# First transform stage of the convolution kernels on four 64x64 tiles of TensorE

## Chip, cores, metric

One core of one Trainium2 chip. The time is device microseconds of one execution, the median of several runs; it is lower when better. The engines are TensorE (PE; its weight loads are listed apart as PEld), VectorE (DVE), ScalarE (ACT) and GpSimd (POOL); SyncE (SP) issues every DMA. Each engine works through its own list of instructions in order and waits on semaphores of the others.

## What is computed

Two state-space convolutions of the same input, mixed by a gate per time step. Length L = 2048, D = 512 channels, N = 128 states. Cut to what matters:

```python
def reference(A_u, ..., gate_w):
    x = A_u                                             # (1, 2048, 512)
    g = sigmoid((x * gate_w).sum(-1, keepdims=True))
    # A: K[d, l] = Re sum_n C dB exp(dt (A_re + i A_im) l)
    # B: K[d, l] = 2 Re sum_n C dt exp(dt (-exp(log_A_real) + i A_imag) l)
    # each: y = irfft(rfft(K, 2L) * rfft(u, 2L))[:L] + u * Dskip
    a = _A_ref(x, ...)
    b = _B_ref(x, ...)
    return g * a + (1 - g) * b
```

## The kernel before

The channels go in four blocks of 128 (`q`), each in two halves of 64 (`v` = 0 to 7). For each `v` there are eight chunks: 16 channels of one of the two convolutions.

A chunk (`chunk`) makes the tables of exponentials on POOL (lines 647 to 670), sines and cosines on ACT (678 to 680), multiplies them on DVE (686 to 701), and PE contracts over the 128 states (`products`, line 715): per channel 32 x 64 values of the convolution kernel, four channels below each other on 128 partitions. Two chunks fill one PSUM bank of 512 columns; ACT copies it to the tile `K` (738).

`put` (line 751) is then the first stage of the Fourier transform, and the function that the change touches. `K` holds, for each of 8 groups of 64 columns, four channels of 32 rows. The tile `w1` (128 x 2 x 128) holds the 32-point transform four times, block by block: a channel's 32 rows meet only the 32 columns of its own block in each of the two parts `d` (cosines, sines), and everything else in `w1` is zero. Each matmul takes 64 columns of `K` as weights and streams 128 columns of `w1`; the two `d` go to the upper and lower half of the output's partitions. Sixteen matmuls fill a pair of PSUM banks (a tile `sd` of 1024 columns, of which there are three), and two copies on DVE or ACT (line 769) bring them to the transform's tile `F`. Four puts make one `F`; there are 32 puts for the kernels (8 `v` of four). The same function transforms the input itself (16 puts, `stage1_u`, from tiles `U` loaded by DMA).

The second stage is line 785 for the input (its results are copied to `z` at 836 and stored in DRAM, `ud`) and line 800 for the kernels; DVE multiplies the two spectra (883), line 898 is the first stage back (64x64 tiles; copied out at 908 and stored in DRAM, `wt`), and line 950 the last, with the gate in its weights (`wg`). Line 993 sums the gate.

What sets the order: the program's operations are not written in sequence. `Plan.run` orders them by a list schedule with a cost for each operation, a due time (tables `TO`, `LAG`, `FSP`, `AN` and so on), free buffers, and for PE a count of instructions in blocks of 256 (`nbytes`, `IFETCH`); the result is a fixed order for every engine. The bits of `EV` and `EU` say which copy of a put goes to DVE (1) or ACT (0), those of `ZU` and `OE` the same for lines 836 and 961/963.

Of the kernel before, what the change touches and what calls it, by code (L numbers as in the profile page):

```python
# [15 lines left out]
D = 512  # L16
NJ, NS = 32, 64
NV = 8
EV = (206, 37, 9, 69, 20, 76, 130, 96)
EU = (253, 223, 202, 103)  # L20
NQ = 4
NCH = 128
NCK = 16
CHUNKS = ((1, 0), (1, 1), (0, 0), (0, 1), (1, 2), (1, 3), (0, 2), (0, 3))
ZU = (85, 125, 85, 48)
PI = math.pi
TWO32 = 4294967296.0
MAGIC = 12582912.0
# [20 lines left out]
GXD = -5.97  # L49
WLD = 11.63  # L50
LAT = {'T': 0.25, 'A': 0.16, 'V': 0.13, 'G': 0.1, 'D': 1.8}
SWITCH = 0.262
TO = (-3.549, -2.629, 0.024, 2.065, 2.702, 4.345, 4.478, 5.927)
LAG = (-1.572, 1.521, 5.972, -3.631, -5.595, -0.093, -15.199, 4.578)
FSP = (-5.044, 9.977, -10.056, 9.928, 7.18, 10.492, 27.495, -2.472)
FL = (5.005, -9.739, 0.3, -7.997)
YSP = (5.177, -6.259, 8.434, -10.145)
UDS = (-4.854, -10.697, -1.47, -1.248)
USP = (5.775, 19.204, 11.776, -6.458)
GD = -12.752  # L60
GSP = 3.036
GWD = -0.281
TXD = -8.835
TWD = 0.073
UAHEAD = -2.124
UPRE = -5.856
FPRE = -2.78
AN = (-6.526, -8.563, -6.831, -12.505, 1.282, 0.999, -2.599, 15.084)
PT = (-10.796, -0.506, 0.169, -0.007)
PC = (-14.288, -17.548, -13.941, -6.07)  # L70
PO = (-7.807, -2.333, -1.426, 1.94, -2.186, -4.121, 4.064, 1.206)
AO = (3.36, -1.366, 2.265, -0.998, -5.989)
CX = 1.593
CA = 7.577
CV = 6.128
CK = 1.86
CE = 0.094
CS = -1.059
FW = -4.653


def _flat(t):
# [27 lines left out]
class Plan:  # L110
# [6 lines left out]

    def op(self, eng, cost, due, fn, r=(), w=(), func=None, nbytes=0, after=(), hold=()):
        o = Op()
        o.eng, o.cost, o.due, o.fn, o.func, o.nbytes = eng, cost, round(due, 6), fn, func, nbytes  # L120
        o.deps, o.bufs = set(after), []
        for items, wr in ((r, False), (w, True)):
            for it in items:
                b, reg = it if isinstance(it, tuple) else (it, None)
                for p, preg, pw in b.log:
                    if p is not o and (wr or pw) and _meet(reg, preg):
                        o.deps.add(p)
                if wr and reg is None:
                    b.log = []
                b.log.append((o, reg, wr))  # L130
                if b not in o.bufs:
                    o.bufs.append(b)
                    b.left += 1
        o.unit = self.unit
        for b in hold:
            o.bufs.append(b)
            b.left += 1
        self.ops.append(o)
        return o

    def run(self):
# [15 lines left out]
        while n < len(self.ops):  # L157
            nxt = 1e30
            for e in at:
# [76 lines left out]
def gated_s4_mix(ctx: ExitStack, tc: tile.TileContext, ins: dict, out: bass.AP):  # L236
    nc = tc.nc
    V, G, A, T = nc.vector, nc.gpsimd, nc.scalar, nc.tensor
# [7 lines left out]
    op = pl.op  # L246
# [49 lines left out]
    for x in range(2):  # L296
        for i in range(2):
            op(
                "A", 1.0, GXD,
                lambda x=x, i=i: A.copy(  # L300
# [3 lines left out]
                r=[raw_g], w=[(GwB, ((2 * x + i, 2 * x + i + 1),))],  # L304
# [35 lines left out]
    w1 = cst.tile([P, 2, P], F32, tag="w1", name="w1")  # L340
    w1B, w1s = Buf(None), Buf("z")
# [36 lines left out]

    op("V", 0.6, WLD, turn_last, w=[wlB, WB])

# [213 lines left out]
    def chunk(v, i, due):  # L594

        k, g = CHUNKS[i]
        q = v // 2
        d = prm[q]
# [4 lines left out]
        x, E, QD, sn, cs = (Buf(t) for t in ("x", "E", "QD", "sd", "sd"))  # L603
# [5 lines left out]
        if i % 4 == 0:  # L609
# [14 lines left out]
                r=[d["pi"], tmB], w=[gh],  # L624
# [6 lines left out]
                r=[d["fi"]], w=[gh],  # L631
# [3 lines left out]
        def turns():  # L635
# [17 lines left out]
            r=[d["pi"], tmB], w=[(x, h0)],  # L653
# [11 lines left out]
        def above():  # L665
# [9 lines left out]
        e = due + CA  # L675
# [6 lines left out]
        e = due + CV  # L682
# [4 lines left out]
            r=[sn, (E, ((0, 1),)), (E, ((2, 3),))], w=[(QD, h0), (QD, ((2, 3),))],  # L687
# [4 lines left out]
            r=[sn, (E, h1)], w=[(QD, h1)],  # L692
# [6 lines left out]
            r=[cs], w=[(E, ((0, 2),))],  # L699
# [5 lines left out]
        kg, K = kgs[0], Kt[v]  # L705
        ko = 256 * odd

        def products():
# [24 lines left out]
            nbytes=132 if odd else 128,  # L733
# [14 lines left out]

        return b.v("p (h m e) -> p h m e", h=NCH // 2, m=NJ, e=2)

    def put(F, K, items, pos, due, bits):

        B, bs = pair()

        def mms():
            for g in range(8):
                for d in range(2):
                    T.matmul(  # L758
                        bs[g // 4]()[64 * d : 64 * d + 64, 128 * (g % 4) : 128 * (g % 4) + 128],
                        K()[:, 64 * g : 64 * g + 64],  # L760
                        w1[:, d, :],
                        start=True, stop=True,
                    )

        op("T", 1.9, due, mms, r=[items, w1B], w=[B], hold=[F], nbytes=64)
        for h in range(2):

            def evict(h=h, e=V.tensor_copy if bits >> h & 1 else A.copy):
                e(F.t[:, 1024 * pos + 512 * h : 1024 * pos + 512 * h + 512], bs[h]())  # L769

            v1 = bits >> h & 1
            c0 = 32 * pos + 16 * h
            op("V" if v1 else "A", 0.6 if v1 else 0.51, due, evict, r=[B], w=[(F, ((c0, c0 + 16), allm))])

    def ms(ug, y):

# [33 lines left out]
    def stage1_u(q, due):  # L810
        F = Ft["u", q] = Buf("F")
        for h in range(2):
            t = Buf("U")
            for i in range(2):
                op(
                    "D", 0.5, due - UAHEAD, lambda t=t, h=h, i=i: DMA(t.t[:, 512 * i : 512 * i + 512], ins["u1"][q, 2 * h + i]),
                    w=[(t, ((2 * i, 2 * i + 2),))], nbytes=262144, hold=[F],
                )
            for i in range(2):
                put(  # L820
                    F, lambda t=t, i=i: t.t[:, 512 * i : 512 * i + 512], (t, ((2 * i, 2 * i + 2),)), 2 * h + i, due,
                    EU[q] >> 4 * h + 2 * i,
                )

    ulast = []
# [1 line left out]
    def stage2_u(q, due):  # L827

        for ug in range(4):
# [4 lines left out]

            def evict(t=t, b=b, e=V.tensor_copy if ZU[q] >> ug & 1 else A.copy):
                e(
# [3 lines left out]

            v1 = ZU[q] >> ug & 1
            op("V" if v1 else "A", 1.13 if v1 else 1.01, dm, evict, r=[b], w=[t])
# [78 lines left out]
    def final(q, due):  # L921

        for pr in range(2):
# [15 lines left out]
            for b in range(2):  # L939
# [236 lines left out]
```

## Time and profile before

| | us |
|---|---|
| median of 3 runs | 520.14 (516.91 to 524.86) |
| the profiled execution | 514.1 |
| its span, first to last instruction | 511.9 |
| mean granted clock of PE | 0.93 |

The profile is of one execution. Busy time is that of an engine's instructions; matmul ends are modelled, so PE busy is not PE at its peak. "PEclk" is the clock that PE was granted, 1.00 being full. A row "idle before, releaser" tells how long an engine stood still before instructions of a group and whose event ended it; "issue" means that it waited for nothing the profile shows. The chain is followed back from the last instruction, at each step to what released it. The next lines are of the page: busy share in 40 equal slices, in tenths.

```profile
PE   4578798797787998668957898499969969999806
...
POOL 4654598596797899996997999959969999930000
PEclk9999899999868999979978999899989979999958
```

POOL is the fullest from the seventh slice to the 35th; the clock dips in some ten places.

### The profile page before, as it was taken

How to read it: one execution, taken by the hardware profiler on the slowest of the kernel's cores; microseconds unless marked ns; L12 is line 12 of the kernel's file. 1: busy time of each engine (PE TensorE's matmuls, PEld its weight loads, DVE VectorE, ACT ScalarE, POOL GpSimd, SP SyncE). 2: the span in 40 equal slices, each digit the busy share in tenths (PEclk: the TensorE clock that was granted, in tenths of full speed). 3: DMA queues.
4: the chain of work that ended last, by engine and by line, in shares of the span. 5: the costliest groups of instructions: out<-in, count | busy, mean ns of one | idle time of the engine just before them, and what ended most of it. 6: DMA issues, size and time to landing. Idle time of an engine off the chain costs nothing.

```text
span 511.9 us, 22739 instructions
## 1 busy us (share of the span) xinstructions
PE 406.6 (79%) x10096; PEld 363.5 (71%) x10096; DVE 390.8 (76%) x502; ACT 390.9 (76%) x590; POOL 380.8 (74%) x334
## 2 busy tenths in 40 slices
PE   4578798797787998668957898499969969999806
PEld 3577787696677887557846787498858858888706
DVE  5845698879766999979965998969949987965300
ACT  5958679798669988898997888987988877762201
POOL 4654598596797899996997999959969999930000
PEclk9999899999868999979978999899989979999958
DMA  8659968747744254315575565724533686536982
GB/s 307 149 152 271 237 174 238 190 100 184 198 147 127 85 147 142 104 40 151 165 237 191 140 188 156 270 107 108 145 83 86 173 256 213 149 86 186 314 202 85
DMA packets 64512, 85.50 MB, mean 167 GB/s; under 512 B 5792, under 2 KB 38944, under 8 KB 64032
## 3 DMA queue, kind: packets, MB, share of 16 engines
q1 hardware_dynamic: 64416, 84.07, 56.8%
q8 instruction: 79, 1.29, 1.0%
q14 instruction: 17, 0.14, 0.1%
HBM read 50.49 MB, written 33.59 MB: 164 GB/s over the span
## 4 chain that ended last, share of the span: by engine, by line
PE 32%; DVE 21%; DMA 14%; ACT 13%; issue 9%; POOL 8%; SPq 3%; DVEq 0%; ACTq 0%; POOLq 0%
PE sd L758 9%; PE sd L898 5%; PE ps L800 4%; PE ps L715 4%; DVE QD L686 4%; PE ps L950 4%; DVE E L696 3%; DVE z L883 3%; DMA ud<-z 3%; DMA F<-in_c_t 3%; DMA out<-st 2%; PE sd L785 2%; ACT sd L680 2%; DMA U<-in_u 2%; DVE F L769 2%
## 5 line engine op out<-in xcount | busy, mean ns | idle before, releaser
L666 POOL TENSOR_TENSOR E<-AB 128x1024 f32<-128x1024 f32 x64 | 125.4, 1960 | 0.0
L883 DVE TENSOR_TENSOR z<-ps,U 128x1024 f32<-128x1024 f32 x64 | 77.7, 1217 | 21.2 <-PE ps L800 15.3
L898 PE MATMUL sd<-z,Tx 64*64 64x128 f32 x2048 | 71.9, 278 | 22.5 <-DVE z L883 13.3
L647 POOL TENSOR_TENSOR x<-pi,c_tm 128x512 int32<-128x512 int32 x64 | 68.0, 1063 | 25.1 <-ACT sd L680 25.1
L658 POOL TENSOR_TENSOR E<-AB 128x512 f32<-128x512 f32 x64 | 68.7, 1074 | 21.8 <-PE ps L715 12.4
L686 DVE TENSOR_TENSOR QD<-sd,E 128x1024 f32<-128x1024 f32 x64 | 77.8, 1215 | 9.0 <-ACT sd L678 5.0
L715 PE MATMUL ps<-E 128*32 128x64 f32 x2048 | 68.1, 229 | 18.7 <-DVE E L701 8.8
L758 PE MATMUL sd<-w,K 128*64 128x128 f32 x1024 | 71.1, 297 | 11.8 <-ACT K L738 7.0
L696 DVE TENSOR_TENSOR E<-sd,E 128x1024 f32<-128x1024 f32 x64 | 77.7, 1214 | 2.1 <-ACT sd L680 2.0
L800 PE MATMUL ps<-F,Gw 128*128 128x128 f32 x512 | 75.3, 289 | 4.7 <-DVE z L883 3.9
L898 PEld LDWEIGHTS sd<-z,Tx 64*64 64x64 f32 x2048 | 56.5, 134 | 30.8 <-DVE z L883 12.8
L678 ACT ACTIVATE sd<-x 128x1024 f32<-128x1024 int32 x64 | 65.8, 1028 | 13.8 <-DVE QD L691 5.4
L758 PEld LDWEIGHTS sd<-w,K 128*64 128x64 f32 x1024 | 62.9, 150 | 16.5 <-ACT K L738 7.5
L800 PEld LDWEIGHTS ps<-F,Gw 128*128 128x128 f32 x512 | 63.4, 192 | 13.5 <-issue 6.7
L715 PEld LDWEIGHTS ps<-E 128*32 128x32 f32 x2048 | 50.3, 114 | 30.0 <-issue 15.8
L680 ACT ACTIVATE sd<-x 128x1024 f32<-128x1024 f32 x64 | 65.9, 1030 | 6.4 <-DVE QD L691 3.0
L679 ACT ACTIVATE x<-x 128x1024 f32<-128x1024 int32 x64 | 67.8, 1059 | 1.3
L638 POOL TENSOR_TENSOR x<-gh 128x512 int32<-128x512 int32 x64 | 68.6, 1072 | 0.1
L715 PE MATMUL ps<-QD 128*32 128x64 f32 x2048 | 66.6, 226 | 1.0 <-issue 1.0
L908 ACT COPY st<-sd 128x512 f32<-128x512 f32 x60 | 35.2, 587 | 26.5 <-PE sd L898 15.9
L769 DVE COPY F<-sd 128x512 f32<-128x512 f32 x45 | 29.7, 685 | 31.7 <-PE sd L758 25.1
L715 PEld LDWEIGHTS ps<-QD 128*32 128x32 f32 x2048 | 52.1, 115 | 1.2 <-issue 1.2
(109 smaller groups left out, 640.1 us busy)
## 6 DMA issues: line engine op xcount, KB each, us to landing
U<-ud SPq DMA_DIRECT2D x64, 256.0 KB, 4.1
wt<-st SPq DMA_DIRECT2D x60, 256.0 KB, 3.7
F<-wt SPq DMA_DIRECT2D x14, 1024.0 KB, 7.8
ud<-z SPq DMA_DIRECT2D x32, 256.0 KB, 3.6
U<-in_u SPq DMA_DIRECT2D x16, 256.0 KB, 4.8
ud<-z SPq DMA_DIRECT2D x32, 128.0 KB, 3.5
U<-in_uT SPq DMA_DIRECT2D x16, 256.0 KB, 4.0
out<-st SPq DMA_DIRECT2D x16, 256.0 KB, 2.4
```

Source lines behind the costliest of these rows:

```text
L638: G.tensor_tensor(xi()[:, :, 1, :].rearrange("n c (a b) -> n c a b", a=4), t[:, :, 0:4].unsqueeze(3).to_broadcast([P, NCK, 4, 8]), t[:, :, ...
L647: lambda: G.tensor_tensor(xi()[:, :, 0, :], d["piv"]()[:, k, ch, 0].unsqueeze(2).to_broadcast([P, NCK, NJ]), tm[:, 0:NJ].unsqueeze(1).to_b ...
L658: G.tensor_tensor(Ev()[:, :, 0, :].rearrange("n c (a b) -> n c a b", a=4), A1()[:, ca, ::-1].unsqueeze(3).to_broadcast([P, NCK, 4, 8]), BB ...
L666: G.tensor_tensor(Ev()[:, :, 1:3, :].rearrange("n c w t -> n c (w t)"), AA()[:, ca].rearrange("n c w a -> n (c w) a").unsqueeze(3).to_broa ...
L680: op("A", 1.03, e, lambda: A.activation(bv(cs), wv(qv(x)), AF.Sin, bias=HALF_PI, scale=-SCL), r=[x], w=[cs], func="S")
L686: lambda: V.tensor_tensor(ev(QD)[:, :, 0::2, :], bv(sn).rearrange("n w c t -> n c w t"), Ev()[:, :, 0::2, :], ALU.mult),
L696: lambda: V.tensor_tensor(Ev()[:, :, 0:2, :], bv(cs)[:, 0].unsqueeze(2).to_broadcast([P, NCK, 2, NJ]), Ev()[:, :, 0:2, :], ALU.mult),
L715: T.matmul(K4[32 * b : 32 * b + 32, gg, :], ev(QD if w else E)[:, c, 2, :], ev(QD if w else E)[:, c, 0:2].rearrange("n h t -> n (h t)"), s ...
L758: T.matmul(bs[g // 4]()[64 * d : 64 * d + 64, 128 * (g % 4) : 128 * (g % 4) + 128], K()[:, 64 * g : 64 * g + 64], w1[:, d, :], start=True, ...
L800: T.matmul(b.v("p (k m h e) -> p m k h e", k=2, m=4, h=32, e=2)[:, mm], Gw[:, m, :], Fv(F)[:, :, m, :].rearrange("p (k h) e -> p k h e", k=2),
L883: lambda Z=Z, b=b, U=U, y=y: V.tensor_tensor(Z.t.rearrange("p (w k n) -> p w k n", w=2, k=2), b.v("p (k n) -> p k n", k=2, n=256).unsqueez ...
L898: T.matmul(bs[x]()[64 * o : 64 * o + 64, 128 * mp : 128 * mp + 128].rearrange("p (k c) -> p k c", k=2), Tx[p, 1 - w, 8 * ug + 4 * y + 2 * ...
```

## The change

Four things. First, `put` has a form for the kernels (`wide` false) that leaves out the zero blocks: 64 rows of `K` (two channels) against the 64 x 64 block of `w1` that is not zero for them. Per put there are 32 matmuls with 64 rows, 64 weight columns and 64 streamed columns where there were 16 with 128 rows, 64 and 128; the two row halves `h` go to two PSUM banks. Second, each of the two copies then takes one bank, and writes every other run of 64 columns of `F` instead of 512 in a row. The input's puts (`wide` true) stay as they were. Third, the planner's cost of a kernel put goes from 1.9 to 1.05 and its instruction count from 64 to 128, and every cost on PE is multiplied by 1.06 (`PEF`). Fourth, all due times and the bits that deal copies to DVE and ACT are drawn anew, so that the order of all engines changes.

```diff
-EV = (206, 37, 9, 69, 20, 76, 130, 96)
-EU = (253, 223, 202, 103)
+EV = (195, 180, 18, 203, 16, 192, 174, 115)
+EU = (223, 255, 19, 123)
...
-ZU = (85, 125, 85, 48)
+ZU = (81, 119, 86, 56)
...
+PEF = 1.06
...
-OE = (12, 7, 0, 0)
+OE = (12, 7, 8, 8)
...
-LAG = (-1.572, 1.521, 5.972, -3.631, -5.595, -0.093, -15.199, 4.578)
+LAG = (-0.365, 2.001, 8.288, -0.64, -4.356, 1.669, -10.725, 7.648)
...
-        o.eng, o.cost, ... = eng, cost, ...
+        o.eng, o.cost, ... = eng, cost * (PEF if eng == "T" else 1.0), ...
...
-        put(Ft[v], lambda: K.t, K, pos, due + CS, EV[v] >> 2 * pos)
+        put(Ft[v], lambda: K.t, K, pos, due + CS, EV[v] >> 2 * pos, False)
...
             for g in range(8):
-                for d in range(2):
-                    T.matmul(
-                        bs[g // 4]()[64 * d : 64 * d + 64, 128 * (g % 4) : 128 * (g % 4) + 128],
-                        K()[:, 64 * g : 64 * g + 64],
-                        w1[:, d, :],
-                        start=True, stop=True,
-                    )
-
-        op("T", 1.9, due, mms, r=[items, w1B], w=[B], hold=[F], nbytes=64)
+                for h in range(1 if wide else 2):
+                    for d in range(2):
+                        if wide:
+                            T.matmul(
+                                bs[g // 4]()[64 * d : 64 * d + 64, 128 * (g % 4) : 128 * (g % 4) + 128],
+                                K()[:, 64 * g : 64 * g + 64], w1[:, d, :], start=True, stop=True,
+                            )
+                        else:
+                            T.matmul(
+                                bs[h]()[64 * d : 64 * d + 64, 64 * g : 64 * g + 64],
+                                K()[64 * h : 64 * h + 64, 64 * g : 64 * g + 64],
+                                w1[64 * h : 64 * h + 64, d, 64 * h : 64 * h + 64],
+                                start=True, stop=True,
+                            )
+
+        op("T", 1.9 if wide else 1.05, due, mms, ..., nbytes=64 if wide else 128)
...
-                e(F.t[:, 1024 * pos + 512 * h : 1024 * pos + 512 * h + 512], bs[h]())
+                f = F.t[:, 1024 * pos : 1024 * pos + 1024]
+                if wide:
+                    e(f[:, 512 * h : 512 * h + 512], bs[h]())
+                else:
+                    e(f.rearrange("p (g h x) -> p g h x", g=8, h=2)[:, :, h], bs[h]().rearrange("p (g x) -> p g x", g=8))
```

How the order moves, at three places. In these lists a row is a run of like instructions with their number; `sd_102` and the like are a buffer and its copy, `64x128` is the output of one matmul, and line numbers after 747 are about 1 to 15 higher in the changed kernel (758 becomes 761 for the input and 766 for the kernels, 769 becomes 779 and 781, 785 becomes 800, 800 becomes 815, 898 becomes 913).

PE at the start, before: from the input's second load to the first products of the tables (line 715).

```order
L758 MATMUL sd_101<-w_114,U_83 64x128 x16
L758 MATMUL sd_100<-w_114,U_83 64x128 x16
L785 MATMUL sd_101<-F_66,Gw 128x2x64 x8
L785 MATMUL sd_102<-F_67,Gw 128x2x64 x8
L715 MATMUL ps_98<-E_73 32x64 x4
L715 MATMUL ps_98<-QD_76 32x64 x4
```

The same place after.

```order
L761 MATMUL sd_101<-w_114,U_83 64x128 x16
L761 MATMUL sd_100<-w_114,U_83 64x128 x16
L800 MATMUL sd_102<-F_66,Gw 128x2x64 x8
L800 MATMUL sd_101<-F_67,Gw 128x2x64 x8
L800 MATMUL sd_100<-F_67,Gw 128x2x64 x8
L800 MATMUL sd_101<-F_67,Gw 128x2x64 x8
L716 MATMUL ps_98<-E_73 32x64 x4
L716 MATMUL ps_98<-QD_76 32x64 x4
```

Two more groups of the input's second stage stand ahead of the first products, and the last of them writes `sd_101`, which the second has to be copied out of.

PE behind the last products, before: the last kernel's last put and the start of its second stage.

```order
L725 MATMUL ps_98<-dskip,c_id 128x8
L898 MATMUL sd_100<-z_80,Tx 64x128 x16
L758 MATMUL sd_101<-w_114,K_79 64x128 x16
L800 MATMUL ps_99<-F_66,Gw 128x2x64 x4
L800 MATMUL ps_98<-F_67,Gw 128x2x64 x4
L898 MATMUL sd_102<-z_81,Tx 64x128 x16
L800 MATMUL ps_99<-F_67,Gw 128x2x64 x4
L898 MATMUL sd_100<-z_80,Tx 64x128 x16
L950 MATMUL ps_98<-F_68,wg 32x128 x32
```

And after.

```order
L726 MATMUL ps_98<-dskip,c_id 128x8
L913 MATMUL sd_101<-z_81,Tx 64x128 x16
L766 MATMUL sd_102<-w_114,K_79 64x64 x32
L815 MATMUL ps_99<-F_67,Gw 128x2x64 x4
L815 MATMUL ps_98<-F_66,Gw 128x2x64 x4
L913 MATMUL sd_100<-z_80,Tx 64x128 x16
L815 MATMUL ps_99<-F_66,Gw 128x2x64 x4
L913 MATMUL sd_101<-z_81,Tx 64x128 x16
L965 MATMUL ps_98<-F_68,wg 32x128 x32
```

Here nothing moved but the put itself: 32 matmuls of 64x64 in place of 16 of 64x128.

DVE at the last chunks, before: copies of puts (769) among the tables' products (686 to 701).

```order
L769 COPY F_67<-sd_102 128x512
L686 TENSOR_TENSOR QD_77<-sd_100,E_73 128x16x2x32
L691 SCALAR_TENSOR_TENSOR QD_77<-sd_100,E_73 128x16x32
L701 TENSOR_TENSOR E_73<-sd_102,E_73 128x16x32
L696 TENSOR_TENSOR E_73<-sd_102,E_73 128x16x64
L883 TENSOR_TENSOR z_80<-ps_99,U_82 128x1024
```

And after.

```order
L692 SCALAR_TENSOR_TENSOR QD_76<-sd_100,E_75 128x16x32
L781 COPY F_66<-sd_101 128x8x64 x2
L702 TENSOR_TENSOR E_75<-sd_102,E_75 128x16x32
L697 TENSOR_TENSOR E_75<-sd_102,E_75 128x16x64
L976 COPY st_85<-ps_99 128x512
L687 TENSOR_TENSOR QD_77<-sd_100,E_73 128x16x2x32
L781 COPY F_66<-sd_101 128x8x64 x2
L898 TENSOR_TENSOR z_80<-ps_99,U_82 128x1024
```

DVE now takes both copies of a put one after the other, between the products of one chunk, and an output copy (976) stands among them.

More of the change, by code (lines that the diff above doesn't have):

```diff
@@ L45 @@
 BW = 290e3
+PEF = 1.06
 IFETCH = 4.0
 PO0, PO1 = 1.03, 1.27
-OE = (12, 7, 0, 0)
-GXD = -5.97
-WLD = 11.63
+OE = (12, 7, 8, 8)
+GXD = -4.913
+WLD = 15.254
 LAT = {'T': 0.25, 'A': 0.16, 'V': 0.13, 'G': 0.1, 'D': 1.8}
 SWITCH = 0.262
-TO = (-3.549, -2.629, 0.024, 2.065, 2.702, 4.345, 4.478, 5.927)
-LAG = (-1.572, 1.521, 5.972, -3.631, -5.595, -0.093, -15.199, 4.578)
[L55 to L79, printed above, removed]
+TO = (-3.701, -0.433, 1.14, 1.333, 3.894, 4.267, 6.651, 6.614)
+LAG = (-0.365, 2.001, 8.288, -0.64, -4.356, 1.669, -10.725, 7.648)
+FSP = (-1.25, 11.409, -8.977, 10.712, 10.421, 11.624, 25.017, -3.233)
+FL = (3.894, -14.374, 2.197, -7.623)
+YSP = (10.309, -8.145, 3.559, -4.359)
+UDS = (-9.201, -10.303, -3.318, -3.254)
+USP = (10.164, 16.637, 13.38, -2.203)
+GD = -14.047
+GSP = 1.036
+GWD = -6.995
+TXD = -17.629
+TWD = 7.99
+UAHEAD = -1.77
+UPRE = -5.291
+FPRE = -3.468
+AN = (-7.415, -8.807, -7.671, -11.882, 1.86, 0.368, 0.217, 16.005)
+PT = (-14.375, -5.93, 1.022, -7.839)
+PC = (-14.984, -13.234, -14.652, 0.927)
+PO = (-6.807, -2.484, -3.173, 1.838, -4.119, -5.668, 3.754, 5.373)
+AO = (2.344, 1.513, 0.866, -1.612, -7.624)
+CX = 0.469
+CA = 8.039
+CV = 5.89
+CK = 1.942
+CE = -1.189
+CS = -0.625
+FW = -4.682
 def _flat(t):
@@ L119, in op @@
         o = Op()
-        o.eng, o.cost, o.due, o.fn, o.func, o.nbytes = eng, cost, round(due, 6), fn, func, nbytes
+        o.eng, o.cost, o.due, o.fn, o.func, o.nbytes = eng, cost * (PEF if eng == "T" else 1.0), round(due, 6), fn, func, nbytes
         o.deps, o.bufs = set(after), []
@@ L749, in Fv, with put @@
         return b.v("p (h m e) -> p h m e", h=NCH // 2, m=NJ, e=2)
-    def put(F, K, items, pos, due, bits):
+    def put(F, K, items, pos, due, bits, wide):
         B, bs = pair()
@@ L821, in stage1_u @@
                     F, lambda t=t, i=i: t.t[:, 512 * i : 512 * i + 512], (t, ((2 * i, 2 * i + 2),)), 2 * h + i, due,
-                    EU[q] >> 4 * h + 2 * i,
+                    EU[q] >> 4 * h + 2 * i, True,
                 )
```

8 lines of the change are left out of this document (6 added, 2 removed).

## The prediction

> **What bounds the kernel now.** I read the page's head first, then busy time by stage, then the chain of work that ended last, then single stretches of PE's timeline.
>
> ```profile
> span 511.9 us, 22739 instructions
> PE 406.6 (79%) x10096; PEld 363.5 (71%) x10096; DVE 390.8 (76%) x502; ACT 390.9 (76%) x590; POOL 380.8 (74%) x334
> ...
> 0.00:64.00 64.00, 42.85 (x606) 40.45 (x608) 38.62 (x75) 46.67 (x83) 35.16 (x42) 0.95 0.80 223
> ...
> 160.00:448.00 288.00, 240.54 (x6346) 212.05 (x6347) 252.02 (x304) 249.66 (x375) 265.06 (x224) 0.93 0.50 150
> 448.00:512.00 64.00, 44.72 (x1113) 40.05 (x1108) 20.14 (x20) 17.89 (x29) 4.00 (x4) 0.89 0.61 174
> ```
>
> The stage rows give, after the stretch, busy time of PE, its weight loads, DVE, ACT and POOL, then PE's granted clock. No engine is full. In the long middle stage POOL has 265 of 288 us (92%), DVE 88%, ACT 87%, PE 84%. Only after 448 us, when POOL has almost nothing left, PE is alone the busiest. So an engine that gets cheaper pays only where it stands on the chain:
>
> ```profile
> PE 32%; DVE 21%; DMA 14%; ACT 13%; issue 9%; POOL 8%; SPq 3%; DVEq 0%; ACTq 0%; POOLq 0%
> ...
> L758 PE MATMUL sd<-w,K x1024: 272/273/473, 96.6 to 460.8; 128*64 128x128 f32 x171
> ...
> 96.63 1.99 PE sd L758 x32
> ...
> 139.36 3.63 PE sd L758 x32
> ...
> 459.17 1.92 PE sd L758 x32
> ```
>
> Line 758 is the first stage; its matmuls on the kernels run from 96.6 us on (on the input before). The last rows are pieces of the chain: start, length, what. From 96.63 on, 16 of the pieces that the chain's answer lists are kernel transforms of 32 records (one put each); they sum to 39.4 us. Eleven took 1.90 to 2.17 us, five 3.27 to 3.70 us, at a halved clock. That is 55% of what those 32 puts keep PE busy (71.1 us, below).
>
> **The put.** Before: 16 matmuls, 32 records (each float32 matmul shows as two), 128 moving columns, two 128x64 tiles. After: 32 matmuls, 64 records, 64 columns, four 64x64 tiles. The columns streamed per put halve, and the instructions double. No row shows a 64x64 tile with 64 columns; these are nearest:
>
> ```profile
> 306.71 1.97 PE L758 MATMUL sd<-w,K 128*64 128x128 f32 x32
> 308.61 0.71 PE L427 MATMUL sd<-c_id,dt_t 128*128 128x128 f32 x4
> 309.25 0.32 PE L715 MATMUL ps<-E 128*32 128x64 f32 x8
> ...
> 310.28 1.97 PE L758 MATMUL sd<-w,K 128*64 128x128 f32 x32
> ...
> 356.38 1.16 PE L800 MATMUL ps<-F,Gw 128*128 128x128 f32 x8
> 357.47 1.10 PE L898 MATMUL sd<-z,Tx 64*64 64x128 f32 x32
> 358.50 0.32 PE L715 MATMUL ps<-E 128*32 128x64 f32 x8
> ...
> 144.32 0.74 PE L993 MATMUL sd<-gate_w,U 128*32 128x1 f32 x64
> ```
>
> From start to next start an old put takes 308.61 - 306.71 = 1.90 us. Line 715 runs 64 records of 64 columns on four 128x32 tiles in 310.28 - 309.25 = 1.03 us, 16 ns a record. Line 898 runs 32 records of 128 columns on four 64x64 tiles, the same columns in all as a new put, also in 358.50 - 357.47 = 1.03 us, but 32 ns a record. If the columns set the pace, a new put takes 1.03 us; if each pair of weight load and matmul in a 64x64 tile needs line 898's 32 ns, it takes 64 x 32 = 2.06 us. I take 1.03: two different forms with equal columns per tile agree on it, and line 715 shows that 64 records fit. Both ends are kept. Gain per put 0.87 us, 46%; on 32 puts 28 us of PE at full clock, and on the chain's 39.4 us 0.458 x 39.4 = **18.0 us**, the half-clock ones in proportion.
>
> The Trainium skill ("TensorE: Matmul & The Clock Gate", the section on 56 against 53.3 ns) says that matmuls never start closer than about 25 ns however few columns they have, a rule against cutting 128 columns to 64. By it a put would be 64 x 25 = 1.6 us, an estimate, and the chain would gain 6 us, not 18. The trace disagrees: line 715 has 16 ns a record, and line 993, with one column, 0.74 us for 64.
>
> **Instructions for PE.** Each put adds 32 records and as many weight loads: 32 x 64 = 2048 instructions on 20192. They come by DMA:
>
> ```profile
> q8 instruction: 79, 1.29, 1.0%
> ...
> 138.19 1.08 PEld L993 LDWEIGHTS sd<-gate_w,U 128*32 128x32 f32 x70 [2.26 <-issue]
> 147.12 0.15 PEld L715 LDWEIGHTS ps<-QD 128*32 128x32 f32 x7 [1.16 <-issue]
> 159.50 0.11 PEld L715 LDWEIGHTS ps<-E 128*32 128x32 f32 x1 [2.75 <-issue]
> ...
> 138.19:147.10 8.91, 7.41 (x254) 0.67 0.46 144
> 147.12:159.49 12.37, 9.69 (x383) 0.72 0.49 156
> ...
> 136.02 2.17 issue
> ...
> 156.91 2.59 issue
> ...
> 407.99 1.81 issue
> ```
>
> 79 packets for 20192 instructions is 256 each, 128 pairs. PE stopped for "issue" at 138.19, 147.12 and 159.50, with 254 and 383 records between, two and three packets: 4.5 and 4.1 us a packet where PE outruns its supply. So 128 pairs that run in under about 4 us stall. Cutting PE's order after every 128 pairs and adding the durations above (line 800: 357.47 - 356.38 = 1.09 us for 8 records), 34 of 79 packets are short of 4 us before, by 23.6 us together; after, 57 of 87, by 56.6. The order now has 64-record puts beside 64-record products of line 715, a packet in 2.1 us. Stalls grow somewhere between nothing (PE idles 105 us anyway) and all 33 us. I take the share that today's chain shows: its three large issue pieces, 2.17 + 2.59 + 1.81 = 6.6 us, over 23.6 us of shortfall is 0.28; times 33 is **+9.2 us**.
>
> **Evictions, and the bits that deal them out.**
>
> ```profile
> L769 DVE COPY F<-sd 128x512 f32<-128x512 f32 x45 | 29.7, 685 | 31.7 <-PE sd L758 25.1 <-ACT F L769 6.5
> L769 ACT COPY F<-sd 128x512 f32<-128x512 f32 x51 | 28.5, 587 | 23.6 <-DVE F L769 15.2 <-PE sd L758 8.1
> ...
> L908 ACT COPY st<-sd 128x512 f32<-128x512 f32 x60 | 35.2, 587 | 26.5 <-PE sd L898 15.9 <-DMA wt<-st 6.3 <-DMA out<-st 3.9
> ...
> L758 PE MATMUL sd<-w,K 128*64 128x128 f32 x1024 | 71.1, 297 | 11.8 <-ACT K L738 7.0 <-ACT F L769 1.5 <-DVE E L696 1.1
> ```
>
> Each copy now writes 8 runs of 64 with gaps between. Line 908 writes runs of 128 at the same 587 ns as the unbroken copy, so I put it at 0. Counting bits, 52 F copies are DVE's after against 45 and ACT has 44 against 51; two output copies (of like size) move the same way. DVE +9 x 0.685 = 6.2 us, ACT -9 x 0.587 = 5.3 us. By their chain shares (21% and 13%) that is +0.6 us. PE's copies wait less: 33 us of eviction waits name line 758, and they shrink with the put, but that is the same 18 us.
>
> **Order at head and tail.** Ahead of the first products stand two more input groups of line 785 (1.9 us each), and the last of them needs a z eviction that DVE did at 47.66.
>
> ```profile
> 71.79 1.89 PE sd L785 x16
> ...
> 47.66 1.23 DVE L836 COPY z<-sd 128x1024 f32<-128x1024 f32 x1 [0.61 <-DMA ud<-z]
> ...
> 45.92 1.07 POOL L658 TENSOR_TENSOR E<-AB 128x512 f32<-128x512 f32 x1 [4.93 <-PE ps L715]
> ...
> 54.39 1.06 POOL L647 TENSOR_TENSOR x<-pi,c_tm 128x512 int32<-128x512 int32 x1 [5.48 <-ACT sd L680]
> ```
>
> POOL waits for those products until 45.92; some 5 us later would end POOL's step near 54, where it then waits for ACT until 54.39 today. The cover is that wait; if ACT gets there sooner, up to 5 us show. I take 0, bounds -2 and +5. Behind the last products PE has the same groups in the same order, 33.5 us of work before and 32.6 after: the tail gains one put, already counted.
>
> **Sum.** 514.1 us (profiled execution; its span is 511.9) - 18.0 + 9.2 + 0.6 = 505.9. The median of the runs shown, 520.14 (516.91 to 524.86), is 6.0 us above that execution, so I shift by 6: 511.9, say **511 us**, 1.8% below the median. What is late next is PE's supply of instructions, then POOL with 8% of gaps left in the middle.
>
> **Rivals.**
> 1. The supply costs nothing on the path, since the new order meets packets where PE idles: 514.1 - 18 + 6 = 502. For it: PE idles 21% of the span. Against: the 16 ns records of two groups side by side.
> 2. Not what it says: 64x64 pairs pace at 32 ns. The put takes 2.06 us, the chain's 39.4 us grow by 8%, +3.3: 524. For it: line 898 never ran faster. Against: its 128 columns explain that.
> 3. The supply decides, on the other side: the whole 33 us of shortfall lands on the path: 514.1 - 18 + 33 + 6 = 535. It is slower by 2% from 28 us of the 33 on. For it: issue pieces already are 9% of the chain. Against: the big ones sum to 6.6 us.
> 4. The clock takes it back:
>
> ```profile
> 323.00:326.40 3.40, 0.00 (x0) 0.00 (x0) 3.19 (x9) 3.35 (x4) 3.40 (x3) 1.00 0.96 351
> 326.40:329.80 3.40, 0.00 (x0) 0.00 (x0) 3.30 (x8) 3.39 (x10) 3.40 (x5) 0.78 1.02 418
> 329.80:333.20 3.40, 3.28 (x86) 3.05 (x90) 2.30 (x3) 3.40 (x12) 3.16 (x4) 0.50 0.33 130
> 333.20:336.60 3.40, 3.40 (x96) 3.25 (x92) 0.69 (x1) 3.37 (x7) 1.67 (x2) 0.72 0.16 58
> ```
>
> After two idle stretches PE worked at 0.50 and 0.72: 3.4 x (0.50 + 0.28) = 2.7 us lost. A PE with 28 us less to do idles more; three more such places on the path are +8: 519. The Trainium skill (same page, "What's actually happening") has the clock halve after an idle window of about 3.4 us; by that rule, the trace agrees.
>
> **How the numbers follow.** The sum's case (504 to 518 with the head's bounds and the spread of the runs) 0.50, of which 0.22 lie below 509.7, 2% under the median; rival 1 0.20, all faster; rival 2 0.08, 0.07 within; rival 3 0.12, slower; rival 4 0.10, 0.09 within. 2% is about what a measurement of this kernel tells from no change. Faster 0.22 + 0.20 = 0.42; within 0.28 + 0.07 + 0.09 = 0.44; slower 0.01 + 0.12 + 0.01 = 0.14. The range 498 to 527 leaves out rival 3 and the fringe of rival 1.
>
> **What would show it.** The put: start to next start of a kernel put near 1.03 us at clock 1.00 (2.06 for rival 2), and the row of its matmuls near 38 us busy, not 71. The supply: 87 packets, and "issue" waits of PE's weight loads well above today's. The clock: mean granted clock under 0.93. POOL's first wait for line 715's products ending later than 46 us while the one on ACT ends near 54 shows the head right. I am wrong if the put is not near 1.03 us, or if kernel puts still hold 9% of the chain.

## The result, and the profile after

The changed kernel takes 532.97 us, median of four runs (531.76 to 537.12), where the kernel before took 519.34 us (516.91 to 524.86) beside it: a ratio of 1.029, 95% interval 1.021 to 1.038. It is slower. The forecast was 511 us, with 527 us as the upper end. All ratios here leave out executions more than 1.5% above the fastest of the same kernel, so they are not quotients of the medians given beside them. The profiled execution of the changed kernel took 534.0 us, and that of the kernel before 514.1, which lies 5 us under its median: of the 20 us between the two profiles about 15 are the change's.

The head of the page of the changed kernel, and the line of the chain (line 766 is the kernel put):

```profile
span 532.2 us, 24797 instructions
PE 404.8 (76%) x11120; PEld 361.0 (68%) x11120; DVE 396.9 (75%) x511; ACT 385.4 (72%) x581; POOL 381.0 (72%) x334
...
PEclk9989899798655999879995898879989986999967
...
q8 instruction: 87, 1.43, 1.1%
...
PE sd L913 5%; PE ps L965 5%; PE ps L815 4%; PE ps L716 3%; DVE z L898 3%; DVE E L697 2%; DMA F<-wt 2%; DMA out<-st 2%; DVE QD L687 2%; PE sd L766 2%; ACT sd L679 1%; ACT st L923 1%; DVE E L702 1%; DVE QD L692 1%; DMA U<-ud 1%
```

PE's busy time falls by under 2 us although the puts lost 28 us, since other work ran at a lower clock (line 898, 913 in the changed kernel, went from 71.9 to 79.7 us): the mean is 0.88 against 0.93, and the clock row (40 slices of 13.3 us) has 6, 5, 5 in slices 11 to 13, where before it had 8, 6, 8, and a new 5 in slice 22, which is looked at below. The chain could be followed back only to 276 us, so its shares, which are of the whole span, leave out the first half.

Busy time by stage (stretch, then PE, weight loads, DVE, ACT, POOL, granted clock, DMA share, GB/s):

```profile
0.00:64.00 64.00, 42.56 (x584) 40.64 (x584) 40.59 (x77) 46.31 (x81) 34.68 (x42) 0.92 0.80 225
...
160.00:448.00 288.00, 221.10 (x6603) 194.08 (x6593) 241.52 (x295) 235.29 (x356) 252.16 (x214) 0.87 0.48 143
448.00:512.00 64.00, 53.01 (x1540) 45.90 (x1536) 40.47 (x44) 29.67 (x41) 20.31 (x17) 0.98 0.63 183
```

In the middle stage every engine does less per microsecond than before: POOL 252 of 288 us against 265, DVE 242 against 252. No engine has become the bound; all of them stand still more often. What POOL, DVE and ACT didn't finish there stands in the next row: POOL has 20 us after 448, where it had 4.

The put itself, from the groups of instructions and from PE's timeline:

```profile
L766 PE MATMUL sd<-w,K 64*64 64x64 f32 x2048 | 42.9, 236 | 15.0 <-ACT K L739 5.3 <-DVE pi L451 3.2 <-DVE E L697 1.5
...
L781 ACT COPY F<-sd 128x512 f32<-128x512 f32 x36 | 19.8, 585 | 13.3 <-PE sd L766 7.3 <-DVE F L781 6.0
...
L781 DVE COPY F<-sd 128x512 f32<-128x512 f32 x28 | 18.4, 685 | 10.5 <-ACT F L781 5.3 <-PE sd L766 5.2
```

It does what it says: 42.9 us busy where there were 71.1, and from start to next start 264.41 - 263.30 = 1.11 us (rows further down). Copies in runs of 64 take 585 ns on ACT and 685 on DVE, where unbroken ones took 587 and 685.

The waits (who, for whom; us together, times, longest):

```profile
PEld ps L716 <- issue: 34.2, 33, 7.7
DVE z L898 <- PE ps L815: 32.5, 18, 5.4
...
POOL E L659 <- PE ps L716: 30.1, 12, 11.4
...
PE ps L716 <- issue: 19.1, 12, 3.4
```

The same four of the kernel before:

```profile
PEld ps L715 <- issue: 17.0, 38, 2.8
DVE z L883 <- PE ps L800: 15.3, 12, 3.8
POOL E L658 <- PE ps L715: 12.4, 8, 4.9
PE ps L715 <- issue: 7.1, 4, 2.6
```

PE stood still for instructions in the tables' products more than twice as long as before (19.1 against 7.1 us, its weight loads 34.2 against 17.0), and DVE and POOL waited twice as long for PE. That reads like rival 3, the supply, but a wait is not yet a cause. The clock is also lower, and the order is another one. The experiments take these apart.

### The profile page after: what moved, and what is told of

It is laid out like the page before. It is cut to its first block, busy times and chain, and to the rows that moved or that the text cites. A ratio compares the mean times of both kernels' runs of the same rounds, so it can differ in the third digit from the quotient of the medians.

```text
span 532.2 us, 24797 instructions
## 1 busy us (share of the span) xinstructions
PE 404.8 (76%) x11120; PEld 361.0 (68%) x11120; DVE 396.9 (75%) x511; ACT 385.4 (72%) x581; POOL 381.0 (72%) x334
## 5 line engine op out<-in xcount | busy, mean ns | idle before, releaser
L913 PE MATMUL sd<-z,Tx 64*64 64x128 f32 x2048 | 79.7, 293 | 31.7 <-DVE z L898 12.3
L913 PEld LDWEIGHTS sd<-z,Tx 64*64 64x64 f32 x2048 | 62.1, 142 | 42.0 <-issue 9.6
L716 PE MATMUL ps<-E 128*32 128x64 f32 x2048 | 72.9, 237 | 19.8 <-issue 8.3
L815 PE MATMUL ps<-F,Gw 128*128 128x128 f32 x512 | 81.7, 305 | 7.5 <-DVE z L898 3.8
L815 PEld LDWEIGHTS ps<-F,Gw 128*128 128x128 f32 x512 | 69.1, 207 | 16.9 <-issue 9.7
L716 PE MATMUL ps<-QD 128*32 128x64 f32 x2048 | 72.4, 234 | 10.8 <-issue 10.8
L716 PEld LDWEIGHTS ps<-QD 128*32 128x32 f32 x2048 | 55.7, 120 | 12.3 <-issue 12.2
L766 PE MATMUL sd<-w,K 64*64 64x64 f32 x2048 | 42.9, 236 | 15.0 <-ACT K L739 5.3
L766 PEld LDWEIGHTS sd<-w,K 64*64 64x64 f32 x2048 | 38.1, 148 | 19.7 <-ACT K L739 5.9
L965 PE MATMUL ps<-F,wg 128*32 128x128 f32 x1024 | 35.5, 304 | 13.2 <-DMA F<-wt 11.1
```

The lines of the kernel that those rows point to most:

```text
L716: T.matmul(K4[32 * b : 32 * b + 32, gg, :], ev(QD if w else E)[:, c, 2, :], ev(QD if w else E)[:, c, 0:2].rearrange("n h t -> n (h t)"), s ...
L766: T.matmul(bs[h]()[64 * d : 64 * d + 64, 64 * g : 64 * g + 64], K()[64 * h : 64 * h + 64, 64 * g : 64 * g + 64], w1[64 * h : 64 * h + 64, ...
L815: T.matmul(b.v("p (k m h e) -> p m k h e", k=2, m=4, h=32, e=2)[:, mm], Gw[:, m, :], Fv(F)[:, :, m, :].rearrange("p (k h) e -> p k h e", k=2),
L913: T.matmul(bs[x]()[64 * o : 64 * o + 64, 128 * mp : 128 * mp + 128].rearrange("p (k c) -> p k c", k=2), Tx[p, 1 - w, 8 * ug + 4 * y + 2 * ...
```

## The experiments

Each was timed beside runs of the kernel before on the same chip; ratios are to those, with 95% intervals, and 1% is 5.2 us.

**1 and 2: the two halves of the change.** Experiment 1 is the kernel before with the put and its copies in the new form, the planner's old tables and old costs kept, so that no engine's order differs but for the put's own rows (the second hunk is against the changed kernel):

```diff
-        put(Ft[v], lambda: K.t, K, pos, due + CS, EV[v] >> 2 * pos)
+        put(Ft[v], lambda: K.t, K, pos, due + CS, EV[v] >> 2 * pos, False)
...
-        op("T", 1.9 if wide else 1.05, due, mms, ..., nbytes=64 if wide else 128)
+        op("T", 1.9, due, mms, ..., nbytes=64)
```

> The new put in exactly the old order of every engine (the planner is given the old cost and count, so only the put's matmuls and its copies' target differ). If the redrawn order is what costs: faster than before, by up to the 18 us that kernel puts hold of the chain, ratio 0.965 to 0.99. If the put's doubled instructions cost it (PE starved, its clock at half for longer): no gain or a loss, ratio 1.00 to 1.03, with granted clock under 0.91 and PE's weight loads waiting for issue well above before.

Experiment 2 is the other half: the changed kernel's tables and costs, but the matmuls and copies of the old put:

```diff
-                for h in range(1 if wide else 2):
+                for h in range(1):
...
-                        if wide:
+                        if True:
...
-                if wide:
+                if True:
```

> The old put in exactly the new order. If the redrawn order costs: slower than the changed kernel, since each put is 0.8 us longer again, ratio 1.03 to 1.06 to before. If the put's instructions cost: close to before, ratio 0.99 to 1.01, granted clock back near 0.93.

Experiment 1 took 526.07 us (519.82 to 528.34, ten runs), 1.009 (1.004 to 1.014). Experiment 2 took 520.59 us (518.38 to 524.65, ten runs), 1.007 (1.003 to 1.011). Each half costs under one per cent, and together they cost three: the new put is slower than the old one in the old order too, by less, and the new order is not what costs 15 us by itself.

**3: extra instructions by themselves.** The kernel before, with a matmul of one column ahead of each of a kernel put's 16:

```diff
                 for d in range(2):
+                    if extra:
+                        o = 64 * d + 32 * (g % 2)
+                        T.matmul(
+                            bs[g // 4]()[o : o + 32, 128 * (g % 4) : 128 * (g % 4) + 1],
+                            K()[:, 64 * g : 64 * g + 32], w1[:, d, 0:1], start=True, stop=True,
+                        )
```

> Before, with 16 more matmuls of one column and 32 weight columns in each kernel put (their output is overwritten at once): as many PE instructions as the changed kernel, order unchanged, and about 0.37 us more PE time a put by the row of line 993 (64 records in 0.74 us). If instructions alone matter little: 55% of 32 x 0.37, up to +6.5 us, ratio 1.00 to 1.013. If the supply of instructions decides: +13 us or more, ratio above 1.02, and longer waits for issue.

It took 734.03 us, 1.416 (1.406 to 1.426): a miss, since it measured something else. PE's timeline of it, at full clock:

```profile
123.34 0.22 PE L760 MATMUL sd<-w,K 128*32 128x1 f32 x2
123.49 0.43 PE L764 MATMUL sd<-w,K 128*64 128x128 f32 x2
123.85 0.22 PE L760 MATMUL sd<-w,K 128*32 128x1 f32 x2
124.00 0.43 PE L764 MATMUL sd<-w,K 128*64 128x128 f32 x2
124.37 0.22 PE L760 MATMUL sd<-w,K 128*32 128x1 f32 x2
```

One extra and one real matmul take 124.37 - 123.85 = 0.52 us, where a real one took 1.90 / 16 = 0.12 before. Every matmul here has another tile form than its neighbour, so 0.4 us go to two changes, 0.2 us each, and 1024 changes make 205 of the 215 us that were lost. Nothing follows on the supply. (Whether the form or the shared output columns cost it, the run does not separate.)

**4 and 5: is PE's time in the puts worth anything, or does a PE with less to do lose its clock?** Both leave out every second group of a kernel put, and so half of its time and half of its instructions. The edit, of the kernel before (4) and of the changed one (5):

```diff
-            for g in range(8):
+            for g in range(0, 8, 2):
```

> Before, with every second of the eight column groups left out of the kernels' puts (half of that transform isn't computed): half the put's PE time and half its instructions, order unchanged. This is the put's time saved without the price in instructions. If kernel puts really hold 39 us of the path, and the supply of instructions ate the gain: faster by up to 18 us, ratio 0.965 to 0.98. If shorter puts only lead into another wait that is as late (POOL, DVE and ACT in a ring): ratio 0.99 to 1.00.

> The changed kernel with every second column group left out of the kernels' puts (half of that transform isn't computed): as many instructions as the old put, half the PE time of the new one, the new order. If the doubled instructions cause what the new put costs in the new order (about 12 us): like the old put in the new order or faster, ratio 0.99 to 1.01 to before. If a PE with too little to do loses its clock, whatever the instructions: as slow as the changed kernel, ratio 1.02 to 1.04, granted clock under 0.90.

Experiment 4 took 515.07 us (511.78 to 519.88), 0.991 (0.987 to 0.995); experiment 5 took 516.90 us (514.07 to 519.69), 0.995 (0.991 to 0.998). Two things follow. Half of the put's time is worth 0.9%, 4.7 us, with the instructions halved as well: the forecast's 18 us aren't there. And experiment 5 has the least work for PE and a mean clock of 0.90, under the 0.93 of before, and is faster than before. So a PE that idles more and has a lower clock need not make the kernel slower.

**6, 7 and 10: the gate's matmuls, which share the supply.** 168 of the 256 matmuls of line 993 are left out, in the kernel before (6) and in experiment 1's kernel (7, and again 10):

```diff
+                                    if q and a + b:
+                                        continue
```

> Before, with 168 of the gate's 256 one-column matmuls left out (part of the gate's sum isn't computed), all its waits kept: 672 instructions fewer, between about 130 and 162 us. The arm to compare the next one with. If the supply is what holds that stretch: the clock there comes back sooner and the kernel is faster by 2 to 6 us. If not: under 1.5 us, which is part of the gate's own 7 us of PE time.

> The new put in the old order, with the same part of the gate left out. If the 5 us that the new put costs there come from the supply in the gate's stretch (clock at 0.50 from 143 to 170 us): that spell is gone and the kernel is level with the gate-cut old put, within 1 us or 0.2%. If they come from elsewhere: still 4 to 6 us slower than it.

> The new put in the old order with part of the gate left out once more, since its first four times lay 27 us apart. Expected as before: level with the gate-cut old put (519.7 us) if the supply in the gate's stretch is where the new put loses its 5 us; 4 to 6 us slower if not.

Experiment 6 took 519.73 us, 1.003 (1.000 to 1.007): 672 instructions fewer and no gain. Experiment 7's four runs lay between 512 and 539 us, too far apart for a ratio. As experiment 10 the same kernel took 525.57 us, 1.008 (1.003 to 1.014), against 1.009 of experiment 1. Taking 672 instructions out of the stretch where the kernel before showed its longest stops for instructions (2.17 us up to 138.19, 2.59 up to 159.50) made neither kernel measurably faster. Whether the new put loses its 5 us there is not decided: against experiment 6 it costs 1.008 - 1.003, or 2.5 us (±3.5), between the two forecasts.

**8 and 9: the same put with half the instructions.** This is the experiment that decides. The four 64x64 tiles, the reads, the copies and the order stay, but a put is 16 matmuls of 128 columns in place of 32 of 64, which is nearly the same PE time (at full clock 1.03 us a put against 1.09 to 1.11 in most); every second group's product is wrong. That a wrong product takes the time of a right one is assumed. Of the changed kernel (8) and of experiment 1's (9):

```diff
-            for g in range(8):
+            for g in range(0, 8, 1 if wide else 2):
...
-                                bs[h]()[64 * d : 64 * d + 64, 64 * g : 64 * g + 64],
+                                bs[h]()[64 * d : 64 * d + 64, 64 * g : 64 * g + 128],
...
-                                w1[64 * h : 64 * h + 64, d, 64 * h : 64 * h + 64],
+                                w1[64 * h : 64 * h + 64, d, :],
```

> The changed kernel, with 16 matmuls of 128 columns in a kernel put in place of 32 of 64, on the same four 64x64 tiles (every second group's columns get a wrong product): by line 898's row the same 1.03 us of PE time, in the same order, with half the instructions. If the number of instructions costs: ratio 0.99 to 1.01 to before, 12 us or more under the changed kernel. If something else in the new put or order does (the tiles, the broken copies, PE idling): 1.02 to 1.035, like the changed kernel.

> The same put of 16 matmuls with 128 columns on 64x64 tiles, in the old order. If the number of instructions costs: ratio 0.985 to 0.995, like the half put of experiment 4, some 9 us under the new put in the old order. If it doesn't: near 1.009, like the new put.

Experiment 8 took 513.47 us (509.85 to 515.52, four runs), 0.988 (0.979 to 0.997); experiment 9 took 513.46 us (509.70 to 515.75, ten runs), 0.990 (0.986 to 0.993). The put in the groups of instructions of experiment 8:

```profile
L766 PE MATMUL sd<-w,K 64*64 64x128 f32 x1024 | 39.6, 298 | 16.4 <-ACT K L739 4.9 <-DVE E L697 4.1 <-DVE pi L451 3.2
```

Its waits for instructions in the products:

```profile
PEld ps L716 <- issue: 23.3, 43, 7.7
...
PE ps L716 <- issue: 4.5, 6, 1.5
```

The puts keep PE busy 39.6 us where the changed kernel has 42.9, and what it no longer has is 2048 of the 24797 instructions and many of the waits for them: PE's own fall from 19.1 to 4.5 us, those of its weight loads from 34.2 to 23.3. The six kernels in one table (ratio to before):

| a kernel put | old order | new order |
|---|---|---|
| 16 matmuls, 1.90 us | 1 (before) | 1.007 (2) |
| 16 matmuls, 1.03 us | 0.990 (9) | 0.988 (8) |
| 32 matmuls, 1.09 to 1.11 us | 1.009 (1) | 1.029 (changed kernel) |

Down from the first row to the second the put's time changes, by 0.87 us in each of 32, and with it the tiles and the copies' target; the instructions stay: -1.05% or 5.5 us in the old order (interval ±2.0), -1.9% or 9.9 us in the new (±5.0; half-widths are added in quadrature), two gains that do not differ within their intervals. Down to the third row the instructions of a put double: +2.0% or 10.2 us (±3.3) in the old order, +4.15% or 21.5 us (±6.3) in the new. The put is also 0.06 to 0.08 us longer there, 2 to 3 us on 32 puts; at the worth of PE time in the step before, that is about 1 us at most. So the number of instructions is the cause of the loss, in both orders. By quotients of the medians this step is 11.6 and 18.3 us, so how much the orders differ is less sure than that both lose.

**11 and 12: where in the new order?** A place stands out in the trace. PE's timeline of the changed kernel (start, length, what; in brackets the idle time before and what ended it):

```profile
263.30 1.18 PE L766 MATMUL sd<-w,K 64*64 64x64 f32 x64
264.41 0.32 PE L716 MATMUL ps<-E 128*32 128x64 f32 x8
...
275.23 0.22 PE L716 MATMUL ps<-E 128*32 128x64 f32 x1
278.89 0.33 PE L716 MATMUL ps<-E 128*32 128x64 f32 x4 [3.44 <-issue]
...
279.48 2.08 PE L815 MATMUL ps<-F,Gw 128*128 128x128 f32 x8
282.93 1.99 PE L913 MATMUL sd<-z,Tx 64*64 64x128 f32 x32 [1.37 <-DVE z L898]
284.84 2.07 PE L815 MATMUL ps<-F,Gw 128*128 128x128 f32 x8
288.32 1.98 PE L913 MATMUL sd<-z,Tx 64*64 64x128 f32 x32 [1.41 <-DVE z L898]
...
293.72 1.99 PE L913 MATMUL sd<-z,Tx 64*64 64x128 f32 x32 [1.41 <-DVE z L898]
```

And its busy time in the two stretches:

```profile
275.00:280.00 5.00, 1.56 (x50) 1.28 (x40) 0.65 (x2) 4.98 (x13) 5.00 (x5) 0.72 0.89 271
280.00:298.00 18.00, 13.81 (x153) 11.77 (x155) 9.12 (x10) 9.03 (x11) 8.96 (x8) 0.51 0.53 165
```

In the middle of a product, with 49 of its 64 records done, PE gets no instructions for 3.44 us while the DMA engines are 89% busy. That it waits for instructions is in the trace's records of the queue q8: in all eight stops of the changed kernel that are longer than 1.2 us, PE goes on 1.40 to 1.54 us after a packet of 16 KB on that queue has landed. At this stop the packet took 1.02 us, less than the mean of 1.10 us of the 87 packets, but it started only at 276.34, 0.9 us after PE had run out, and 7.85 us after the packet before it. It was late, not slow; why it started late (the full DMA engines are one candidate) no run shows.

The granted clock falls to half from 277.2 to 297.7 us. What follows is a round in which each waits for the one before it: line 815 on PE, the multiplication of line 898 on DVE, line 913 on PE. At half clock a round takes 288.32 - 282.93 = 5.4 us, 1.4 of them idle, and PE stays at 0.51 for 18 us; POOL stands still half of that. Experiment 8 at the same place:

```profile
272.53 1.10 PE L913 MATMUL sd<-z,Tx 64*64 64x128 f32 x32 [1.37 <-DVE z L898]
273.56 1.16 PE L815 MATMUL ps<-F,Gw 128*128 128x128 f32 x8
276.13 1.10 PE L913 MATMUL sd<-z,Tx 64*64 64x128 f32 x32 [1.41 <-DVE z L898]
```

No stop, full clock, 3.6 us a round with the same 1.4 us idle. Experiment 11 therefore puts the wide form into the eight puts of `v` = 3 and 4 alone, which lie around this place, and experiment 12 into the 24 others:

```diff
-        put(Ft[v], lambda: K.t, K, pos, due + CS, EV[v] >> 2 * pos, False)
+        put(Ft[v], lambda: K.t, K, pos, due + CS, EV[v] >> 2 * pos, False, 2 if v in (3, 4) else 1)
...
-            for g in range(8):
+            for g in range(0, 8, gs):
...
-                                bs[h]()[64 * d : 64 * d + 64, 64 * g : 64 * g + 64],
+                                bs[h]()[64 * d : 64 * d + 64, 64 * g : 64 * g + 64 * gs],
...
-                                w1[64 * h : 64 * h + 64, d, 64 * h : 64 * h + 64],
+                                w1[64 * h : 64 * h + 64, d, :] if gs == 2 else w1[64 * h : 64 * h + 64, d, 64 * h : 64 * h + 64],
```

> The changed kernel, but the puts of v = 3 and v = 4 (8 of 32, the ones before and in the stretch from 240 to 320 us) have the 16 matmuls of 128 columns of experiment 8; every second group's product is wrong in these eight puts. All 32 such puts gave back 19.5 us. Theory of one place (a stop for instructions at 276 us in the products, after which PE stays at half clock in a ring of DVE, PE and PE): these eight puts alone give back the step of about 9 us between chunks 34 and 36, 524 us or below, and no round of 5.4 us is seen near 280 us. Rival, the cost is spread evenly over the instructions: a quarter of 19.5 us, 528 us, and the step at 36 stays or turns up elsewhere.

> The other 24 puts in the form of 16 matmuls of 128 columns (every second group's product wrong in them), v = 3 and 4 in the changed kernel's form. Theory of one place: at most 11 of the 19.5 us come back, 522 to 524 us. Rival, spread evenly: three quarters, 15 us, 518 us. If both this kernel and the one before it come near 514 us, the stop at 276 us hangs on chance of phase and not on the puts near it.

Experiment 11 took 527.66 us (520.80 to 532.25), 1.015 (1.008 to 1.022): 1.4% or 7.5 us given back (±5.6). Experiment 12 took 522.48 us (518.88 to 529.53), 1.009 (1.006 to 1.012): 10.7 us given back (±4.7). The times do not decide, since both intervals hold both forecasts. At the place itself the traces are plainer. Experiment 11:

```profile
269.36 1.10 PE L766 MATMUL sd<-w,K 64*64 64x128 f32 x32 [0.93 <-ACT K L739]
...
273.69 0.26 PE L716 MATMUL ps<-E 128*32 128x64 f32 x4 [2.03 <-issue]
...
277.39 1.98 PE L913 MATMUL sd<-z,Tx 64*64 64x128 f32 x32 [1.37 <-DVE z L898]
...
282.68 1.10 PE L913 MATMUL sd<-z,Tx 64*64 64x128 f32 x32 [1.41 <-DVE z L898]
...
286.28 1.10 PE L913 MATMUL sd<-z,Tx 64*64 64x128 f32 x32 [1.41 <-DVE z L898]
```

And experiment 12 (its profiled execution took 529.5 us, 7 above its median, so only this place is read from it):

```profile
267.06 1.16 PE L766 MATMUL sd<-w,K 64*64 64x64 f32 x64 [0.94 <-ACT K L739]
...
273.33 0.33 PE L716 MATMUL ps<-E 128*32 128x64 f32 x4 [3.98 <-issue]
...
277.37 1.98 PE L913 MATMUL sd<-z,Tx 64*64 64x128 f32 x32 [1.38 <-DVE z L898]
...
282.76 1.98 PE L913 MATMUL sd<-z,Tx 64*64 64x128 f32 x32 [1.41 <-DVE z L898]
...
287.85 1.10 PE L913 MATMUL sd<-z,Tx 64*64 64x128 f32 x32 [1.41 <-DVE z L898]
```

With the new puts around it the stop is 3.4 and 4.0 us, the clock stays at half for 20.5 and 13.7 us, and PE runs three and two rounds; with the wide ones it is 2.0 us, 6.8 us at half clock and one round. I had said that no round of 5.4 us would be left; one was. Its price can be read on POOL: between the same two table products (those that start at 269.2 and 285.1 us before) the changed kernel takes 299.8 - 277.7 = 22.1 us and experiment 12 takes 20.9; experiment 11 takes 16.6, experiment 2 14.0 and experiment 8 12.9. So this place holds some 6 to 9 of the 21.5 us.

The rest can be followed on POOL too, since each pair of kernels runs the same table products in the same order. How far the kernel with 32 matmuls a put lies behind the one with 16, in us, where the two table products around the place start and at the end:

| | product at 269.2 (before) | product at 285.1 | end of the span |
|---|---|---|---|
| new order: changed kernel behind experiment 8 | 4.9 | 14.0 | 18.6 |
| old order: experiment 1 behind experiment 9 | 3.4 | 3.8 | 9.0 |

In these profiled executions the one place makes the difference between the orders, 9.1 us against 0.4; outside of it both lose about the same, 9.5 and 8.6 us, mostly in small steps. They are single executions, and others differ from them by some us.

No kernel here that computes the whole of the reference was faster than the kernel before; one with 16 matmuls of useful 128-column products on these tiles was not tried.

## Why the prediction was wrong

In the order that was made the terms came out at -9.9 us for the shorter put, +21.5 for the instructions and +3.6 for the new order with its dealing of copies, +15.2 together (the steps of one table, so they add up by construction), where the forecast had -18.0, +9.2, and +0.6 and 0 for copies and order, or -8.2.

**The step that failed by most: the +9.2 us for instructions.** Its size was right for the old order (10.2 ± 3.3 us, experiments 9 and 1), and wrong for the order that was made (21.5 ± 6.3, experiments 8 and the changed kernel). "I take the share that today's chain shows", 0.28 of the shortfall, carries a share over from one order to another, and the shortfall itself comes out the same, to within 1 us, in the old and in the new order. Counting short packets told how long PE would be starved, not whom it would keep waiting. The stop at 275 us shows the missing part: it fell ahead of the groups of line 815 that DVE waits for (POOL in turn stood still 5.15 us for ACT and 3.72 for DVE behind it), and the clock stayed at half for 20.5 us. Rival 3 had the time (535) at a chance of 0.12, by luck: its 33 us of stalls and its 18 us of gain are both too large, and the two errors cancel. The bound that it was "slower by 2% from 28 of the 33 us on" needed that saving of 18 us.

**The -18.0 us.** This is the second term that failed. The same saving of PE time was worth 5.5 us (±2.0) in the old order and 9.9 (±5.0) in the new. Sixteen puts did stand on the chain with 39.4 us, but the chain names only who was last, not by how much; most of what the puts gave up went to other waits. That POOL was busy for 265 of the middle stage's 288 us stood in the prediction as a fact beside the sum, and it is the likely limit: experiment 9 has 265.5 us there, and from the table product at 60.0 us to the one at 445.0 it takes 383.4 us where the kernel before takes 385.0. (The profiled execution of before lies 5 us under its median, so its middle may be longer in others.) That POOL is what holds the middle was not tested by itself. The prediction's two signs of being wrong did not show this: the put is near 1.03 us, and kernel puts hold 2% of the span on the chain, not 9%, though only the chain's second half could be followed. They test the saving on PE, not what it is worth.

**The order at head and tail, at 0.** The new order alone, all of it, costs 3.6 us (experiment 2; 1.4 to 5.7), about the upper half of the bounds of -2 and +5. The cover that I named, POOL's wait for ACT until 54.39, did not hold. POOL's timeline of the changed kernel:

```profile
52.78 1.07 POOL L659 TENSOR_TENSOR E<-AB 128x512 f32<-128x512 f32 x1 [11.36 <-PE ps L716]
...
62.11 1.06 POOL L648 TENSOR_TENSOR x<-pi,c_tm 128x512 int32<-128x512 int32 x1 [0.88 <-ACT sd L681]
...
64.16 1.95 POOL L667 TENSOR_TENSOR E<-AB 128x1024 f32<-128x1024 f32 x1
```

POOL waited until 52.78, not 45.92, which is 6.9 us later; the table product that stood at 60.01 came at 64.16, so 4.1 of them remained. That was not lost for good: six products later the changed kernel was 4.1 us ahead (106.4 against 110.5).

**What was right.** The put: 1.11 us against 1.03, and 42.9 us busy against about 38. Line 715's 16 ns a record carried over (64 records in 1.11 us are 17 ns), rival 2's 32 ns did not. Nor did the 25 ns of the Trainium skill ("TensorE: Matmul & The Clock Gate", the section on 56 against 53.3 ns). 87 packets, as counted. The evictions at 0.6 us were not tested apart; their durations came as taken.

**Rival 4, the clock.** The clock was lower, as it says, but a PE with less to do isn't the cause: experiments 4, 5, 8 and 9 give it still less, and are faster than before. The half clock is part of how one stop at 275 us costs more than its 3.4 us.

## What to carry to other kernels

When an engine's instructions come in packets that take longer to arrive than to run, count instructions as a resource of their own: a form that halves the streamed columns and doubles the matmuls here lost 10 us in one order and 21 in another, while the same saving of PE time without them won 5.5 and 9.9. A share of the chain is what a shorter step could give, not what it gives: here 18 us were forecast from it and 5.5 and 9.9 came, beside an engine that is busy for 92% of the longest stage. A stall estimate taken from one order need not carry to another; look for the places where starved stretches meet work that others wait for.

## What the runs showed of the hardware

- Stops for instructions of 3.4 to 4.0 us in the middle of a row of short matmuls, and 2048 instructions on 22749 that cost 10 to 21 us. In the changed kernel PE went on 1.40 to 1.54 us after a packet of 16 KB had landed on the instruction queue, in eight stops of eight. The Trainium skill ("Runtime: NRT & Kernel Launch", "Instruction fetch mechanics") has the crossing from one block of 256 instructions to the next as mostly hidden; on PE with 17 ns a record it wasn't here, and the measurement decides.
- Matmuls of alternating tile forms (128x32 and 128x64) that write shared columns cost some 0.2 us at each change, about 205 us for 1024 of them; form and shared columns were not separated.
- Half clock outlasts the stop that it follows: behind stops of 2.0, 4.0 and 3.4 us it stayed for 6.8, 13.7 and 20.5 us, through rounds of 5.1 to 5.4 us with 1.4 us idle, where the same round at full clock, with the same 1.4 us idle in 3.6, stayed at full.
- The mean granted clock is no measure of time: the ten executions of experiment 9 had 0.90 to 0.91 and took 510 to 516 us, the 19 of the kernel before beside them 0.92 to 0.93 and 515 to 525 us.
